# Moving a quarter of the first batch's turns and last transforms in among the first token tiles of a fused spectral mixing and feed-forward kernel

## The chip, the cores and the metric

The kernel runs on one core of one Trainium2 chip. The metric is the device time of one execution in microseconds (us). Before the change it is 847.4 us.

## The reference

There are two parts. The first transforms each of 8 batches of 3008 x 256 values along the sequence, multiplies by a complex 256 x 256 matrix, thresholds softly and transforms back. The second puts each of the resulting 24064 tokens through a feed-forward layer.

```python
X = np.fft.rfft(x, axis=1)
Yr = Xr @ w_r - Xi @ w_i + b_r          # Yi likewise
Yr = np.sign(Yr) * np.maximum(np.abs(Yr) - lam, 0.0)
y = np.fft.irfft(Y, n=x.shape[1], axis=1)
# ... y, as 24064 tokens of 256, is x of the second part
h = x @ w_in                            # 256 -> 2048
r = np.maximum(h, 0.0)
g = s * (r * r) + b
return (g @ w_out).astype(np.float32)   # 2048 -> 256
```

Since b is one number, b times the column sums of `w_out` is a vector of 256 that is added to each token. The kernel computes it once and calls it the bias.

## The kernel before

The transforms are matrix products on TensorE, whose results an eviction (`evac`) copies from a PSUM bank to SBUF. A running sum of estimated costs decides whether ScalarE or VectorE gets each eviction. Batch 0 goes first and alone. From then on the token tiles run, and the transforms of the next batch are laid between their matmuls by a plan of slots, 16 to a tile.

At the end of batch 0 stand the turns (a transposition by matmul, tile `vs`) and the last DFT (tile `yt`, which is what the token tiles read). `ec` is one of two halves of the 256 features, and the 32 values of `n2` go in groups.

```python
        # end of first_batch, for ec = 1
        for k in range(4):
            turn(1, k)                    # 8 values of n2: 8 matmuls, 2 evictions
            some(1)                       # one piece of batch 1's first DFT (tile u)
            if k:
                last_dft(1, 8 * (k - 1))
        last_dft(1, 24)
        return more
    # ...
    schedule(0, 10, more)
    plan.setdefault(15, []).append(make_bias)
    plan.setdefault(17, []).append(load_x_2)
```

A pair of slots of a token tile is four matmuls of 512 columns, a relu on ScalarE (tile `rt`) and a square (tile `gt`), mostly on VectorE. The gt then feed the second product (`psa`, then `ost`).

```python
        rt = rpool.tile([P, 2, 512], F32, name="rt", tag="rt")      # 3 buffers
        nc.scalar.activation(out=rt[:, :, 0:w], in_=ps[:, :, 0:w], func=AF.Relu)
        # ...
            nc.vector.tensor_tensor(
                out=gt[:, :, 0:w], in0=rt[:, :, 0:w], in1=rt[:, :, 0:w], op=ALU.mult
            )
```

The bias needs the sum of `w_out` over its 16 row blocks. GpSimd adds them in SBUF, eight operations in a row, once `w_out` has come from memory. `make_bias` is one matmul with ones and two evictions.

```python
    def emit_load_weights():
        for dc in range(DC):
            nc.gpsimd.dma_start(out=w_in_t[dc], in_=moe_w_in[dc * P : (dc + 1) * P, :])
        nc.gpsimd.dma_start(
            out=w_out_t, in_=moe_w_out.rearrange("(mc p) d -> p mc d", p=P)
        )
    # ...
    def sum_w_out():
        acc = opool.tile([P, 2, D], F32, name="acc", tag="ost")
        nc.gpsimd.tensor_tensor(
            out=acc, in0=w_out_t[:, 0:2], in1=w_out_t[:, 2:4], op=ALU.add
        )
        for q in range(4, MC, 2):
            nc.gpsimd.tensor_tensor(out=acc, in0=acc, in1=w_out_t[:, q : q + 2], op=ALU.add)
        nc.gpsimd.tensor_tensor(out=w_sum, in0=acc[:, 0], in1=acc[:, 1], op=ALU.add)

    def make_bias():
        ps = other_bank()
        nc.tensor.matmul(ps[:, 0:D], ones, w_sum, start=True, stop=True)
        # ... two evictions with scale b
```

Of the kernel before, what the change touches and what calls it, by code (L numbers as in the profile page):

```python
# [14 lines left out]
P = 128  # L15
# [81 lines left out]
def kernel(  # L97
# [13 lines left out]
    nc = tc.nc  # L111
# [7 lines left out]
    HW = N2 // 2  # L119
# [45 lines left out]
    def evac(dst, src, cols, scale=None):  # L165
        ta, td = 0.17 + cols / 1200.0, 0.15 + cols / 960.0
        if load["act"] + ta <= load["dve"] + td:
            load["act"] += ta
            if scale is None:
                return None, nc.scalar.copy(out=dst, in_=src)  # L170
            return None, nc.scalar.mul(out=dst, in_=src, mul=scale)
        load["dve"] += td
        if scale is None:
            return nc.vector.tensor_copy(out=dst, in_=src), None
        return nc.vector.tensor_scalar_mul(out=dst, in0=src, scalar1=scale), None
# [3 lines left out]
    def mix_bank():  # L179
        return pools["m"].tile([P, 512], F32, name="psm", tag="psm")  # L180
# [3 lines left out]
    def any_bank():  # L184

        turn_of[0] += 1
        if "h" in pools:
            return (other_bank, one_bank)[turn_of[0] % 2]()
        return (mix_bank, one_bank, mix_bank, other_bank)[turn_of[0] % 4]()
# [4 lines left out]
    def one_bank():  # L194
        return fpool.tile([P, 512], F32, name="psf", tag="psf")

    def other_bank():
        return apool.tile([P, 512], F32, name="psa", tag="psa")
# [54 lines left out]
    eye_t = cpool.tile([P, P], F16, name="eye_t")  # L253
# [102 lines left out]
    vs = {}  # L356
# [6 lines left out]
    def first_batch():  # L363
# [3 lines left out]
        for g in range(N2 // 4):  # L367
            c, h = divmod(g, 2)
            for dc in range(DC):
                ps = one_bank() if dc else mix_bank()  # L370
                with tc.issue_after(last_pe.ins):
                    for j in range(4):
# [4 lines left out]
                            start=True, stop=True,  # L377
# [35 lines left out]
        vt = bigpool.tile([P, DC, N2, 96], F16, name="vt", tag="corr")  # L413
# [3 lines left out]
        def mix(ec, u):  # L417

            g = vpool.tile([P, 4, 2, P], F16, name="g0", tag="v")
            gs[(ec, u)] = g  # L420
            for half in range(2):
                ps = mix_bank().rearrange("p (j r e) -> p j r e", j=2, r=2)
                for j in range(2):
                    q = 4 * u + 2 * half + j
                    for dc in range(DC):
                        nc.tensor.matmul(  # L426
                            ps[:, j], ut[:, dc, 4 * q : 4 * q + 4, :],
                            W_t[:, dc, :, ec * P : (ec + 1) * P],
                            start=(dc == 0), stop=(dc == DC - 1),
                        )  # L430
                if half:
                    nc.scalar.copy(out=g[:, 2:4], in_=ps)
                    load["act"] += 0.58
                else:
                    nc.vector.tensor_tensor(
                        out=g[:, 0:2], in0=ps,
                        in1=b_g[:, :, ec * P : (ec + 1) * P].unsqueeze(1).to_broadcast(
                            [P, 2, 2, P]
                        ),
                        op=ALU.add,  # L440
                    )
                    load["dve"] += 0.69
# [27 lines left out]
        def inv_dft(ec, u):  # L470
            ps = other_bank()
            z = zt.pop((ec, u))
            for j in range(4):
                nc.tensor.matmul(
                    ps[:, j * P : (j + 1) * P], z[:, j, :], T_t[:, 4 * u + j, :],
                    start=True, stop=True,
                )
            evac(
                vt[:, ec, :, 16 * u : 16 * u + 16],
                ps.rearrange("p (k n) -> p n k", n=N2), 512,  # L480
            )
# [1 line left out]
        for h in range(2):  # L483
            vs[(0, h)] = vspool.tile([96, HW, D], F16, name="vs", tag="vs")

        def turn(ec, k):
            for i in range(2):
                ps = any_bank() if ec else mix_bank()
                n = 8 * k + 4 * i
                for j in range(4):  # L490
                    nc.tensor.matmul(
                        ps[0:96, j * P : j * P + P], vt[:, ec, n + j, :], eye_t,
                        start=True, stop=True,
                    )
                h, n = divmod(n, HW)
                evac(
                    vs[(0, h)][:, n : n + 4, ec * P : (ec + 1) * P],
                    ps[0:96].rearrange("p (j e) -> p j e", e=P), 512,
                )

        yt = yts[0] = ypool.tile([P, DC, N2, 96], F16, name="yt", tag="yt")

        def last_dft(ec, n2):

            if ec or n2 >= 16:
                ps = [any_bank(), any_bank()]
            else:
                ps = [one_bank(), other_bank()]
            for j in range(8):
                h, k = divmod(n2 + j, HW)  # L510
                nc.tensor.matmul(
                    ps[j // 4][:, (j % 4) * 96 : (j % 4) * 96 + 96],
                    vs[(0, h)][:, k, ec * P : (ec + 1) * P], C_t,
                    start=True, stop=True,
                )
            for i in range(2):
                evac(
                    yt[:, ec, n2 + 4 * i : n2 + 4 * i + 4, :],
                    ps[i][:, 0:384].rearrange("p (j n) -> p j n", n=96), 384,
                )  # L520

        more = s1_units(1, True)

        def some(n):
            for _ in range(n):
                if more:
                    more.pop(0)()

        steps = [(ec, u) for ec in range(DC) for u in range(U)]
        for i in range(2 * U + 2):  # L530
            if i < 2 * U:
                mix(*steps[i])
            if 0 <= i - 1 < 2 * U:
                fwd_dft(*steps[i - 1])
            if 0 <= i - 2 < 2 * U:
                inv_dft(*steps[i - 2])
            k = i - U - 2
            if 0 <= k < 4:
                turn(0, k)
            for n in {1: (0,), 2: (8,), 4: (16, 24)}.get(k, ()):  # L540
                last_dft(0, n)
            if i >= 2 * U:
                some(3)
            if i == 9:

                gate = nc.gpsimd.tensor_copy(out=low[0:1, 0, 0:1], in_=vt[0:1, 1, 0, 0:1])
                with tc.issue_after(gate.ins):
                    make_w_g()
                    make_bounds()
                    sum_w_out()  # L550
        for k in range(4):
            turn(1, k)
            some(1)
            if k:
                last_dft(1, 8 * (k - 1))
        last_dft(1, 24)
        return more


    def s1_units(b, more_banks=False):  # L560

        ud = dpool.tile([96, N2, D], F16, name="ud", tag="ud")
        hold = {}

        def unit(i):
            c, j = divmod(2 * i, XCH)
            if j == 0:
                hold["u"] = upool.tile([P, XCH, D], F16, name="u", tag="u")
            ps = any_bank() if more_banks else one_bank()
            nc.tensor.matmul(  # L570
                ps[0:96, :], A_t[0:N1, :], x16[(b, c)][0:N1, j * D : (j + 2) * D],
                start=True, stop=True,
            )
            u = hold["u"]
            evac(u[0:96, j : j + 2, :], ps[0:96, :].rearrange("p (j d) -> p j d", j=2), 512)
            if j == XCH - 2:
                nc.sync.dma_start(
                    out=ud[:, c * XCH : (c + 1) * XCH, :], in_=u[0:96]
                )
            if i == N2 // 2 - 1:  # L580
                uv = ud.rearrange("k n d -> (k n) d").rearrange("(q p) d -> p q d", p=P)
                for q in range(4):
                    t = uspool.tile([P, 6, D], F16, name="us", tag="us")
                    nc.sync.dma_start(out=t, in_=uv[:, 6 * q : 6 * q + 6, :])
                    us[(b, q)] = t

        return [lambda i=i: unit(i) for i in range(N2 // 2)]
# [273 lines left out]
    plan = {}  # L861

    def schedule(start, span, units):
        for i, u in enumerate(units):
            plan.setdefault(start + (i * span) // len(units), []).append(u)

    with tc.tile_pool(name="psm", bufs=4, space=bass.MemoryType.PSUM) as pool:
        pools["m"] = pool
        more = first_batch()
    pools["h"] = ctx.enter_context(  # L870
        tc.tile_pool(name="psh", bufs=2, space=bass.MemoryType.PSUM)
    )
# [6 lines left out]
        if tl[0] == "main" and tl[2] == 0 or tl[0] == "wide" and tl[2] == (0, 0):  # L879
            mark[tl[1]] = i * MC  # L880
    schedule(0, 10, more)
    plan.setdefault(15, []).append(make_bias)
    plan.setdefault(17, []).append(load_x_2)
    schedule(24, 42, s23_units(1))
    schedule(mark[1] - 12, 16, s4_units(1))
    for b in range(2, B):
        s0, s1, s2 = mark[b - 2], mark[b - 1], mark[b]
        p = s1 - s0
        schedule(s0 + 40, p - 48, s1_units(b))
        p = s2 - s1  # L890
# [47 lines left out]
```

## Time and profile before

| | before |
|---|---|
| device time, median of 6 runs (lowest to highest) | 847.43 us (847.01 to 849.07) |
| first token matmul `psh` | 47.90 us |
| first relu `rt` | 49.10 us |
| first square `gt` | 50.15 us |
| batch 1's second DFT, first matmul `psf<-F_t,us` | 62.91 us |

The last line is a good landmark: everything that the change takes away lies before it, and about two thirds of what it puts in elsewhere (1.00 of 1.56 us of matmul by the prediction's count). A trace's zero is not quite fixed, however. The first turn of `ec` = 1 comes at 41.21 us in this trace, so differences between kernels are taken from that turn on.

The prediction shows the shares of the engines, the busy time by stretch and the chain. This is GpSimd's timeline around the end of batch 0. The columns of a timeline are start and duration in us, engine, line, operation, output<-inputs with shapes, and in brackets the idle time before it with what ended it.

```profile
40.67 1.15 POOL L340 TENSOR_TENSOR acc<-w_out_t 128x512 f32<-128x512 f16 x1 [4.95 <-DMA w_out_t<-in_moe_w_out_dram]
41.90 7.30 POOL L344 TENSOR_TENSOR acc<-acc,w_out_t 128x512 f32<-128x512 f32 x6
49.28 0.72 POOL L345 TENSOR_TENSOR w_sum<-acc 128x256 f16<-128x256 f32 x1
```

GpSimd waits 4.95 us for `w_out`, then adds without a pause and is done at 49.28 + 0.72 = 50.00 us.

### The profile page before, as it was taken

What the parts mean: (1) busy time and instruction counts of PE and PEld (TensorE: products, weight loads), DVE (VectorE), ACT (ScalarE), POOL (GpSimd) and SP (SyncE); (2) the same over time, 40 slices, a digit from 0 to 9 for tenths busy, and PEclk for the clock granted to TensorE, in tenths of its full rate; (3) what the DMA queues carried; (4) which work ended last, traced back from release to release, by engine and by line L of the source; (5) the groups of instructions that cost most, each with busy time, mean ns of one, the idle gap of its engine ahead of it and who ended that gap; (6) DMA issues with size and microseconds to landing.
All of it is one profiled execution on the core that took longest, in us unless ns stands there. A gap on an engine that the chain in (4) does not pass through costs nothing.

```text
span 845.0 us, 17114 instructions
## 1 busy us (share of the span) xinstructions
PE 833.8 (99%) x6653; PEld 599.6 (71%) x6653; DVE 693.6 (82%) x1026; ACT 641.8 (76%) x864; POOL 45.0 (5%) x71
## 2 busy tenths in 40 slices
PE   8999999999999999999999999999999999999997
PEld 6857767777677766777677776777667777766765
DVE  5989987888888987888888888798978888776674
ACT  5988887778778877787777787778877878766673
POOL 5331000000000001000000000000000000000000
PEclk9999999999999999999999999999999999999999
DMA  8945567124752367324761248513354223411111
GB/s 202 180 143 122 121 173 203 57 77 101 203 154 56 101 169 190 92 68 107 189 175 49 81 103 205 160 42 91 113 144 125 64 74 95 112 33 38 38 44 50
DMA packets 105746, 96.06 MB, mean 114 GB/s; under 512 B 9542, under 2 KB 97482, under 8 KB 104322
## 3 DMA queue, kind: packets, MB, share of 16 engines
q1 hardware_dynamic: 99218, 80.55, 33.0%
q0 software_dynamic: 6448, 14.42, 10.6%
q8 instruction: 52, 0.85, 0.4%
q14 instruction: 28, 0.23, 0.1%
HBM read 53.52 MB, written 46.66 MB: 119 GB/s over the span
## 4 chain that ended last, share of the span: by engine, by line
PE 90%; ACT 3%; DMA 3%; DVE 2%; issue 1%; POOL 0%; SPq 0%; ACTq 0%; DVEq 0%; POOLq 0%
PE psa L840 37%; PE psh L769 36%; PE psf L635 4%; PE psf L570 2%; PE psf L621 2%; PE psf L606 2%; PE psf L665 2%; PE psf L718 2%; ACT rt L776 2%; PE psm L426 1%; DMA x<-in_x_dram 1%; DMA ud<-u 1%; DVE gt L783 1%; DMA us<-ud 1%; DMA F_c<-dft_fwd 0%
## 5 line engine op out<-in xcount | busy, mean ns | idle before, releaser
L776 ACT ACTIVATE rt<-psh 128x1024 f32<-128x1024 f32 (+2 forms) x384 | 386.7, 1008 | 119.6 <-PE psh L769 117.5
L783 DVE TENSOR_TENSOR gt<-rt 128x1024 f16<-128x1024 f32 (+2 forms) x322 | 385.7, 1202 | 95.4 <-ACT rt L776 94.5
L840 PE MATMUL psa<-w_out_t,gt 128*128 128x256 f16 (+1 forms) x3024 | 454.4, 272 | 0.1
L840 PEld LDWEIGHTS <-gt 128*128 128x128 f16 (+1 forms) x3024 | 300.9, 101 | 187.0 <-issue 1.4
L769 PE MATMUL psh<-yt,w_in 128*128 128x512 f16 (+1 forms) x1344 | 396.3, 378 | 0.2 <-ACT rt L776 0.2
L769 PEld LDWEIGHTS <-w_in 128*128 128x128 f16 x1536 | 142.8, 98 | 27.3 <-issue 1.8
L850 DVE SCALAR_TENSOR_TENSOR ost<-psa,s_bc,bias_bc 128x512 f32<-128x512 f32 (+2 forms) x97 | 71.1, 733 | 10.0 <-PE psa L840 8.2
L780 ACT ACTIVATE gt<-rt 128x1024 f16<-128x1024 f32 (+2 forms) x62 | 65.3, 1054 | 1.0
L640 DVE TENSOR_TENSOR ring<-psf,s 128x512 f16<-128x512 f32 x84 | 57.5, 685 | 3.8 <-PE psf L635 3.3
L170 ACT CAST v<-psf 128x512 f16<-128x512 f32 x78 | 45.3, 583 | 19.7 <-PE psf L665 19.7
L170 ACT CAST xf<-psf 128x512 f16<-128x512 f32 x82 | 47.9, 586 | 10.9 <-PE psf L606 10.9
L170 ACT CAST u<-psf 96x512 f16<-96x512 f32 x76 | 43.9, 580 | 12.4 <-PE psf L570 12.2
L769 PE MATMUL psh<-tail,w_in 128*128 128x512 f16 (+1 forms) x192 | 52.1, 353 | 0.0
L635 PE MATMUL psf<-W_g,xf 128*128 128x256 f16 x336 | 50.4, 273 | 0.0
L170 ACT CAST yt<-psf 128x480 f16<-128x480 f32 (+2 forms) x73 | 37.8, 525 | 11.6 <-PE psf L718 11.6
L213 POOL DMA_DIRECT2D x<-in_x_dram x36 | 18.7, 526 | 430.3 <-PE psf L570 429.2
L570 PE MATMUL psf<-x,A_t 94*96 94x512 f16 x103 | 39.3, 382 | 1.1 <-ACT yt L170 0.5
L646 DVE TENSOR_TENSOR ring<-ring,high 128x512 f16<-128x512 f16 x84 | 35.6, 423 | 2.3
L647 DVE TENSOR_TENSOR ring<-ring 128x512 f16<-128x512 f16 x84 | 35.5, 423 | 2.0
L645 DVE TENSOR_TENSOR ring<-ring,low 128x512 f16<-128x512 f16 x84 | 35.4, 421 | 1.6
L635 PEld LDWEIGHTS <-xf 128*128 128x128 f16 x336 | 32.9, 98 | 3.8
L718 PE MATMUL psf<-C_t,vs 96*128 96x96 f16 x448 | 33.2, 205 | 0.2 <-ACT yt L170 0.2
(97 smaller groups left out, 499.5 us busy)
## 6 DMA issues: line engine op xcount, KB each, us to landing
out_dram<-ost SPq DMA_DIRECT2D x152, 128.0 KB
ud<-u SPq DMA_DIRECT2D x28, 384.0 KB
us<-ud SPq DMA_DIRECT2D x28, 384.0 KB
vd<-v SPq DMA_DIRECT2D x42, 256.0 KB
vs<-vd SPq DMA_DIRECT2D x14, 768.0 KB
x<-in_x_dram POOLq DMA_DIRECT2D x28, 376.0 KB, 5.9
ring<-ring SPq DMA_DIRECT2D x280, 32.0 KB
out_dram<-ost SPq DMA_DIRECT2D x16, 120.0 KB
```

Source lines behind the costliest of these rows:

```text
L170: return None, nc.scalar.copy(out=dst, in_=src)
L570: nc.tensor.matmul(ps[0:96, :], A_t[0:N1, :], x16[(b, c)][0:N1, j * D : (j + 2) * D], start=True, stop=True,)
L635: nc.tensor.matmul(ps[:, r, :], xt[:, 2 - r, dc], W_g[:, dc, r], start=(dc == 0), stop=(dc == DC - 1),)
L640: nc.vector.tensor_tensor(out=t, in0=ps, in1=hold[i // 2][:, i % 2].unsqueeze(1).to_broadcast([P, 2, D]), op=ALU.add,)
L646: nc.vector.tensor_tensor(out=m, in0=m, in1=high, op=ALU.min)
L718: nc.tensor.matmul(ps[:, j * 96 : (j + 1) * 96], vs[(b, h)][:, k, ec * P : (ec + 1) * P], C_t, start=True, stop=True,)
L769: nc.tensor.matmul(o, w_in_t[dc][:, mc * P : (mc + 1) * P], r, start=(dc == 0), stop=(dc == DC - 1),)
L776: nc.scalar.activation(out=rt[:, :, 0:w], in_=ps[:, :, 0:w], func=AF.Relu)
L780: nc.scalar.activation(out=gt[:, :, 0:w], in_=rt[:, :, 0:w], func=AF.Square)
L783: nc.vector.tensor_tensor(out=gt[:, :, 0:w], in0=rt[:, :, 0:w], in1=rt[:, :, 0:w], op=ALU.mult)
L840: nc.tensor.matmul(ps[0:size, h, :], gts[(ti, mc // 2)][:, mc % 2, sub * size : (sub + 1) * size], w_out_t[:, mc, :], start=(mc == 0), sto ...
L850: nc.vector.scalar_tensor_tensor(out=ost[0:size, 0:k], in0=ps[0:size, 0:k], scalar=s_bc[0:size], in1=bias_bc[0:size, 0:k], op0=ALU.mult, o ...
```

## The change

The intent is to let the token tiles begin earlier. For `ec` = 1 the turns and last DFTs of the second half of `n2` leave the end of batch 0, where the engines that empty PSUM are the bound, and are laid into slots 12 to 31, where TensorE has other matmuls to do. (`schedule(12, 22, rest)` spreads the eight groups over the 22 slots from 12 on.) The bias moves from slot 15 to slot 17.

```diff
-        for k in range(4):
-            turn(1, k)
-            some(1)
-            if k:
-                last_dft(1, 8 * (k - 1))
-        last_dft(1, 24)
-        return more
+        turn(1, 0)
+        turn(1, 4)
+        some(1)
+        turn(1, 8)
+        turn(1, 12)
+        some(1)
+        last_dft(1, 0)
+        last_dft(1, 4)
+        some(2)
+        last_dft(1, 8)
+        last_dft(1, 12)
+
+        rest = []
+        for n in (16, 24):
+            rest += [lambda n=n: turn(1, n), lambda n=n: turn(1, n + 4)]
+            rest += [lambda n=n: last_dft(1, n), lambda n=n: last_dft(1, n + 4)]
+        return rest, more
 ...  (turn and last_dft now do 4 values of n2 a call instead of 8; same matmuls, same evictions)
     schedule(0, 10, more)
-    plan.setdefault(15, []).append(make_bias)
-    plan.setdefault(17, []).append(load_x_2)
+    schedule(12, 22, rest)
+    plan.setdefault(17, []).append(make_bias)
+    plan.setdefault(18, []).append(load_x_2)
```

More of the change, by code (lines that the diff above doesn't have):

```diff
@@ L484, in first_batch, with turn, last_dft @@
             vs[(0, h)] = vspool.tile([96, HW, D], F16, name="vs", tag="vs")
-        def turn(ec, k):
-            for i in range(2):
-                ps = any_bank() if ec else mix_bank()
-                n = 8 * k + 4 * i
-                for j in range(4):
-                    nc.tensor.matmul(
-                        ps[0:96, j * P : j * P + P], vt[:, ec, n + j, :], eye_t,
-                        start=True, stop=True,
-                    )
-                h, n = divmod(n, HW)
-                evac(
-                    vs[(0, h)][:, n : n + 4, ec * P : (ec + 1) * P],
-                    ps[0:96].rearrange("p (j e) -> p j e", e=P), 512,
-                )
+        def turn(ec, n):
+            ps = any_bank() if ec else mix_bank()
+            for j in range(4):
+                nc.tensor.matmul(
+                    ps[0:96, j * P : j * P + P], vt[:, ec, n + j, :], eye_t,
+                    start=True, stop=True,
+                )
+            h, k = divmod(n, HW)
+            evac(
+                vs[(0, h)][:, k : k + 4, ec * P : (ec + 1) * P],
+                ps[0:96].rearrange("p (j e) -> p j e", e=P), 512,
+            )
         yt = yts[0] = ypool.tile([P, DC, N2, 96], F16, name="yt", tag="yt")
-        def last_dft(ec, n2):
-            if ec or n2 >= 16:
-                ps = [any_bank(), any_bank()]
-            else:
-                ps = [one_bank(), other_bank()]
-            for j in range(8):
-                h, k = divmod(n2 + j, HW)
+        def last_dft(ec, n):
+            if ec or n >= 16:
+                ps = any_bank()
+            else:
+                ps = other_bank() if n % 8 else one_bank()
+            for j in range(4):
+                h, k = divmod(n + j, HW)
                 nc.tensor.matmul(
-                    ps[j // 4][:, (j % 4) * 96 : (j % 4) * 96 + 96],
+                    ps[:, j * 96 : j * 96 + 96],
                     vs[(0, h)][:, k, ec * P : (ec + 1) * P], C_t,
@@ L515, in last_dft @@
                 )
-            for i in range(2):
-                evac(
-                    yt[:, ec, n2 + 4 * i : n2 + 4 * i + 4, :],
-                    ps[i][:, 0:384].rearrange("p (j n) -> p j n", n=96), 384,
-                )
+            evac(
+                yt[:, ec, n : n + 4, :],
+                ps[:, 0:384].rearrange("p (j n) -> p j n", n=96), 384,
+            )
         more = s1_units(1, True)
@@ L538, in first_batch @@
             if 0 <= k < 4:
-                turn(0, k)
-            for n in {1: (0,), 2: (8,), 4: (16, 24)}.get(k, ()):
+                turn(0, 8 * k)
+                turn(0, 8 * k + 4)
+            for n in {1: (0, 4), 2: (8, 12), 4: (16, 20, 24, 28)}.get(k, ()):
                 last_dft(0, n)
@@ L868 @@
         pools["m"] = pool
-        more = first_batch()
+        rest, more = first_batch()
     pools["h"] = ctx.enter_context(
```

## The prediction

> **What bounds the kernel now.** First the page's busy shares, then the shares of the chain that ended last.
>
> ```profile
> PE 833.8 (99%) x6653; PEld 599.6 (71%) x6653; DVE 693.6 (82%) x1026; ACT 641.8 (76%) x864; POOL 45.0 (5%) x71
> ...
> PE 90%; ACT 3%; DMA 3%; DVE 2%; issue 1%; POOL 0%; SPq 0%; ACTq 0%; DVEq 0%; POOLq 0%
> ```
>
> TensorE is the bound. The change neither adds nor removes a matmul, so it can only gain what TensorE loses in gaps. The 99% does not show those: a matmul is drawn longer than its turn in the pipeline. I therefore took starts, not lengths, from TensorE's timeline: eight 512-column matmuls from 47.90 to 49.62 us are 0.216 us each, and likewise 0.108 for 256 columns, 0.055 for 128 and 0.0425 for 96. Gap = distance between starts minus these. From 72 to 824 us it comes to 0.6 to 1.5 us per 40 us where no records are missing, mostly rounding. Where batch 0 ends it is denser: 0.8 us in 40.0 to 42.1, 0.3 to 44.3, 1.1 to 46.6, 0.4 to 49.6, 0.4 to 52.0: 3.1 us in 12. From there to 63 us it is near zero. Then the busy time by stretch:
>
> ```profile
> core 0: us, PE busy (x) PEld busy (x) DVE busy (x) ACT busy (x) POOL busy (x), PEclk, DMA share, GB/s
> ...
> 38.00:48.00 10.00, 8.48 (x100) 5.94 (x100) 9.39 (x18) 8.99 (x20) 6.91 (x6) 1.00 0.43 101
> 48.00:59.50 11.50, 11.29 (x59) 5.44 (x57) 10.32 (x11) 10.66 (x15) 1.88 (x2) 1.00 0.56 164
> 59.50:63.00 3.50, 3.50 (x28) 2.47 (x28) 3.14 (x3) 2.04 (x3) 0.35 (x1) 1.00 0.54 141
> 63.00:90.00 27.00, 26.88 (x225) 19.93 (x224) 24.36 (x47) 22.83 (x33) 2.74 (x8) 1.00 0.50 106
> ```
>
> In 38 to 48 us VectorE and ScalarE are 94% and 90% busy emptying PSUM banks; TensorE waits for banks. The chain over that stretch says the same (start, us, what):
>
> ```profile
> 41.89 1.07 ACT vs L170 x2
> 42.96 0.49 ACT u L170
> 43.45 0.38 ACT yt L170
> 43.83 0.49 ACT vs L170
> 44.31 0.49 ACT u L170
> 44.80 0.49 ACT vs L170
> 45.29 0.49 ACT u L170
> 45.77 0.39 ACT yt L170
> 46.20 0.59 PE psa L570 x2
> ...
> 47.70 1.29 DVE u L174 x2
> ...
> 49.10 1.03 ACT rt L776
> ```
>
> Evictions of vs (turns), yt (last DFT) and u (first DFT of batch 1) stand back to back, and the first relu of the token tiles (rt) starts at 49.10. After that VectorE is the tight one for ten products:
>
> ```profile
> 50.15 11.48 DVE L783 TENSOR_TENSOR gt<-rt 128x1024 f16<-128x1024 f32 x10 [1.18 <-ACT rt L776]
> 61.99 1.23 DVE L783 TENSOR_TENSOR gt<-rt 128x1024 f16<-128x1024 f32 x1 [0.36 <-ACT rt L776]
> ```
>
> Tile 0 cannot use its second product freely until its eight gt exist (50.15 + 8 x 1.15 = 59.3 us); from then TensorE is truly the bound, because a pair of slots holds 4 x 0.216 + 8 x 0.108 = 1.73 us of matmul against 1.15 of VectorE and 0.97 of ScalarE.
>
> **What the Trainium skill says.** The page "Perfetto Trace Analysis", section "Identifying the Most-Contended Engine", says matmul busy time is no measure of distance to the roofline, because matmuls are pipelined. This trace agrees: 8.48 of 10 us busy in 38 to 48 while the starts leave 2.8 us of gap. "TensorE: Matmul & The Clock Gate", section "Wait — 56ns, not 53.3ns?", gives 55.6 and 215.7 ns start to start at 128 and 512 columns; the trace has 55 and 215 to 216. "PSUM — Partial Sum Buffer", section "Engine vs sequencer instructions", says the queues of ScalarE and VectorE are strict FIFO and matmuls start in program order. So a bank that waits behind other evictions holds up TensorE, and an eviction moved among the tokens delays every gt behind it. The trace's 11.48 us block of gt, and TensorE's longest wait here (0.52 us before 46.20, for ScalarE's yt), fit that.
>
> **The change part by part.** Moved: for the second half of e and n2 = 16 to 31, four turns and four last-DFT groups: 16 matmuls of 0.055 and 16 of 0.0425, 0.88 + 0.68 = 1.56 us of TensorE, and 8 evictions. An eviction's turn on its engine (distance between starts) is 0.60 (vs) or 0.46 us (yt) on VectorE and 0.48 or 0.38 on ScalarE. Splitting the two functions into groups of four changes no count.
>
> *Taken from the end of batch 0.* I compared the built instruction orders. VectorE's list from 43.94 us on was 2 vs, 4 yt, 2 u (4.25 us) and becomes 3 u, 1 yt (2.26). ScalarE loses 2 vs, 1 yt and 1 u (1.8 us). I then walked the new order by hand with the durations above, each bank free when its eviction ends: TensorE reaches the last u at about 45.1, the first token matmul at 45.3 (was 47.90); ScalarE finishes its u at 46.1; four matmuls plus 0.2 us give the first rt at 46.5 (was 49.10). So the token stage starts 2.6 us earlier. TensorE had 1.56 us less to do there, so 2.6 - 1.56 = 1.0 us of gap is gone. Of the 2.6 us, the eviction load explains 1.9 (3.8 us over two engines); the other 0.7 are two bank waits of TensorE (0.28 us for vs, 0.52 us for yt) which lose their cause.
>
> *Put into the token tiles.* Same walk, counted from the first rt. ScalarE and VectorE set the pace of tile 0, and two turns and two last-DFT groups stand between its matmuls. VectorE takes one vs after its fourth gt: counting them from 0, gt 7 ended at about +10.2 (59.3) and ends at +10.8. ScalarE takes a vs and a yt, and the two bias evictions now follow (0.38 + 0.83 us) before rt 8. The 32nd second product of tile 0 came at +13.8 and comes at +14.9: 1.05 later, for 1.00 us of moved matmuls (three turns, two groups) ahead of it. So TensorE pays for almost all that it takes in: the gaps in this stage were already filled with second products. In time from the start: 62.9 becomes 46.5 + 14.9 = 61.4, 1.5 us earlier, with 0.56 us (one turn, two groups) still to come. Net: 1.5 - 0.56 = about 1.0 us.
>
> *Bias at slot 17.* Same matmul and two evictions, later. Its w_sum is ready at 50.0 us; by the walk the matmul stands at 54.9, so no new wait. Its user, the first ost, comes at about 62. Nothing.
>
> *Afterwards.* 63 to 90 us: VectorE was busy 24.4 of 27.0 us (90%), ScalarE 22.8 (85%). Roughly four of the moved evictions (vs and yt on each) land at its beginning, where TensorE loses 0.5 us to an xf that is behind gt and ost; in the new order the same wait remains (0.57 by the walk). I allow 0.1 us more. Expected: 847.4 - 1.0 + 0.1 = 846.5 us.
>
> **Rivals.**
> 1. *The whole advance counts.* If token tiles absorbed the moved matmuls in idle time, the gain would be 2.6 us: 844.8. For it: TensorE has about 0.7 us of gap in 49.6 to 52. Against it: from 52 to 63 starts follow one another with no gap, so there is nothing to absorb 1.56 us.
> 2. *VectorE becomes the bound of tiles 0 to 2.* Its queue is full for 11.5 us and 90% full afterwards; three more evictions (0.60 + 0.60 + 0.46 us) might each appear as delay of gt, then of second products: +1.7 us on top, total about 848. Against it: once tile 0 has its gt, TensorE has 48 second products (5.2 us) in reserve.
> 3. *Banks.* The two psa banks also hold the sums of the second product. A turn or last DFT that takes one must be evicted before the next pair of sub-tiles needs it, and one turn waits for the ost that frees its bank. If these meet badly, 0.5 to 1 us is lost: 847 to 847.5. In the walk ost ends 0.6 us before that turn, which is little.
> 4. *Data.* The fourth chunk of u needs the buffer of the first, whose store to memory is issued at 40.94; the last such store took about 2.6 us to land. It is needed at 45.1 instead of 47.05. If late, half a microsecond goes.
>
> **Range and chances.** The central figure is 846.5. Rivals 2 to 4 push up by 0.3 to 1.5 us, rival 1 down by up to 1.6; balancing of ScalarE against VectorE also differs after the change, so later tiles shift by a few tenths either way. The three runs before spread 0.5 us. Range 845.4 to 847.7. Two per cent is 17 us, more than the whole batch-0 end; faster or slower by that has chance 0.005 each.
>
> **What would show it right or wrong.** First token matmul (psh) at 45.3 and first rt at 46.5 us; VectorE's idle before its first gt similar; the stretch up to it with fewer vs and yt evictions. Batch 1's second DFT (psf<-F_t,us) beginning at 61.4 instead of 62.91, followed by one turn and two groups. TensorE's gaps by starts about 1 us less in 40 to 48 and unchanged after. I am wrong if TensorE shows waits for gt, vs or psa between 50 and 70 us (rivals 2 and 3), if the last u waits (4), or if that second landmark is 2 us or more earlier (1).

## The result, and the profile after

| | before | after |
|---|---|---|
| device time, median of 6 (lowest to highest) | 847.43 us (847.01 to 849.07) | 849.14 us (848.67 to 849.82) |
| ratio, 95% interval | | 1.0019 [1.0006, 1.0032] |

A ratio is the mean time of one kernel's runs over that of the other's of the same rounds, so it is not quite the ratio of the medians. By the 2% measure the two are the same; the interval says that the changed kernel is slightly slower. That is 1.7 us more by the medians, where 0.9 us less was predicted, and outside the range.

The page of the changed kernel, first its busy shares, then the shares of the chain that ended last:

```profile
PE 834.2 (98%) x6653; PEld 599.3 (71%) x6653; DVE 695.9 (82%) x1027; ACT 642.4 (76%) x863; POOL 47.5 (6%) x71
...
PE 91%; DVE 3%; ACT 3%; DMA 1%; issue 1%; POOL 0%; ACTq 0%; DVEq 0%; POOLq 0%
```

The matmuls are the same 6653. GpSimd (POOL) is 2.5 us busier with the same 71 instructions. VectorE (DVE) is 2.3 us busier. Its mix of work has changed a little (1027 instructions instead of 1026), but experiment 1 below has the same 1027 in 693.9 us, so 2.0 us of this is longer durations. The chain holds 3% of DVE instead of 2%.

The stretches of busy time, with the columns of the prediction's table. The cuts are at the first token matmul (45.5), at the first second products and at the landmark (63.60):

```profile
38.00:45.50 7.50, 6.76 (x67) 4.30 (x68) 7.50 (x14) 7.01 (x16) 4.18 (x4) 1.00 0.65 139
45.50:52.50 7.00, 6.83 (x38) 3.34 (x37) 5.58 (x5) 6.37 (x9) 6.36 (x5) 1.00 0.41 125
52.50:63.60 11.10, 9.51 (x66) 5.82 (x66) 10.44 (x10) 8.31 (x13) 3.40 (x7) 1.00 0.56 147
```

The first row ends 2.4 us earlier than before, as intended. The last row is where the loss shows: TensorE is busy 9.51 of 11.10 us, a stretch for which the prediction had near zero gap. VectorE is 94% busy with 10 instructions there. In the second row GpSimd works 6.36 of 7.00 us, until 52.17, and VectorE's gt begin within it, at 47.80; in the kernel before GpSimd had 1.88 us of work from 48 us on, and none from the start of gt at 50.15 to the end of that stretch at 59.5.

The chain from the end of batch 0 on (start, us, what) answers to the one that the prediction shows of before:

```profile
45.71 0.88 PE psh L778 x4
...
46.74 1.03 ACT rt L785
...
47.80 6.59 DVE gt L792 x4
54.39 0.60 DVE vs L174
54.99 4.55 DVE gt L792 x4
...
59.58 0.39 PE psa L849 x2
```

The matmuls and the first relu are where the prediction put them, 46.74 for an expected 46.5. Then four gt take 6.59 us, and the next four 4.55. The path runs straight through VectorE until TensorE at last gets gt for a second product at 59.58. So it is the first four gt that are too long, and each of them can be looked at alone. VectorE's timeline, from narrow windows:

```profile
47.80 1.68 DVE L792 TENSOR_TENSOR gt<-rt 128x1024 f16<-128x1024 f32 x1 [1.43 <-ACT rt L785]
...
49.41 2.17 DVE L792 TENSOR_TENSOR gt<-rt 128x1024 f16<-128x1024 f32 x1
...
51.50 1.75 DVE L792 TENSOR_TENSOR gt<-rt 128x1024 f16<-128x1024 f32 x1
```

And what GpSimd does at that time, first its six additions together, then the last two of them alone, then the last sum:

```profile
42.31 8.19 POOL L344 TENSOR_TENSOR acc<-acc,w_out_t 128x512 f32<-128x512 f32 x6
...
47.25 1.16 POOL L344 TENSOR_TENSOR acc<-acc,w_out_t 128x512 f32<-128x512 f32 x1
...
48.48 2.02 POOL L344 TENSOR_TENSOR acc<-acc,w_out_t 128x512 f32<-128x512 f32 x1
...
50.58 1.59 POOL L345 TENSOR_TENSOR w_sum<-acc 128x256 f16<-128x256 f32 x1
```

An undisturbed gt is 1.22 us long and an undisturbed add 1.15, and the last sum was 0.72 in the kernel before. Read the two lists against each other. The gt at 47.80 begins under the add that ends at 47.25 + 1.16 = 48.41, 0.61 us later. The add at 48.48 ends at 50.50 although it needs only 1.15; the gt that was running ended at 47.80 + 1.68 = 49.48, so it waited 1.00 for it. The gt at 49.41 then stands until that add ends at 50.50, that is 1.09 us, and needs 1.08 more. The sum at 50.58 stands until the gt ends at 51.58, and the gt at 51.50 until the sum ends at 52.17. The two engines take turns, each waiting out what is left of the other's operation. What each gt needs after that is the same: 1.68 - 0.61 = 1.07, then 1.08, then 51.50 + 1.75 - 52.17 = 1.08 us (a little less than the 1.22 of an undisturbed one; why is not shown). That speaks for waiting and against running slowly side by side. The three gt together are (1.68 - 1.22) + (2.17 - 1.22) + (1.75 - 1.22) = 1.94 us too long.

Nothing of this shows as a wait: the operations are drawn longer, as busy time. The waits appear one engine further on. The waits that fit, in 44 to 110 us (total us, times, longest):

```profile
PE psh L778 <- ACT rt L785: 1.2, 4, 0.6
...
ACT rt L785 <- DVE gt L792: 0.9, 2, 0.6
...
PE psa L849 <- DVE gt L792: 0.5, 1, 0.5
```

A late gt keeps one of the three rt buffers, so the next relu starts late, so its PSUM banks are not free for the next psh. By starts, TensorE's gaps are 1.2 us between 51.9 and 54.4 and 0.7 us just before 59.58. The landmark comes at 63.60 instead of the predicted 61.4.

**What the page "SBUF — State Buffer" says of it.** The Trainium skill's section "SBUF: two separate sides" calls the second pair of SBUF interfaces, which VectorE shares with GpSimd, an exclusive lock: a VectorE operation with two SBUF inputs takes it against a GpSimd operation that reads SBUF, and the later one blocks fully. The turns above agree: the add stands 1.00 us and the gt 1.09 us, by the reading above in each case until the other's operation has ended. The prediction had not looked this page up.

### The profile page after: what moved, and what is told of

Read it like the earlier page. It is cut to its first block, busy times and chain, and to the rows that moved or that the text cites. A ratio compares the mean times of both kernels' runs of the same rounds, so it can differ in the third digit from the quotient of the medians. Undisturbed runs are those within 1.5% of the kernel's fastest.

```text
span 847.0 us, 17109 instructions
## 1 busy us (share of the span) xinstructions
PE 834.2 (98%) x6653; PEld 599.3 (71%) x6653; DVE 695.9 (82%) x1027; ACT 642.4 (76%) x863; POOL 47.5 (6%) x71
## 4 chain that ended last, share of the span: by engine, by line
PE 91%; DVE 3%; ACT 3%; DMA 1%; issue 1%; POOL 0%; ACTq 0%; DVEq 0%; POOLq 0%
PE psa L849 37%; PE psh L778 36%; PE psf L644 4%; PE psf L579 3%; PE psf L630 2%; PE psf L615 2%; PE psf L727 2%; PE psf L674 2%; DVE gt L792 2%; ACT rt L785 1%; PE psm L426 1%; DMA x<-in_x_dram 1%; DMA F_c<-dft_fwd 1%; PE psf L456 0%; ACT yt L170 0%
## 5 line engine op out<-in xcount | busy, mean ns | idle before, releaser
L789 ACT ACTIVATE gt<-rt 128x1024 f16<-128x1024 f32 (+2 forms) x64 | 67.3, 1051 | 1.0
L170 ACT CAST u<-psf 96x512 f16<-96x512 f32 x80 | 46.3, 580 | 12.8 <-PE psf L579 12.5
L170 ACT CAST xf<-psf 128x512 f16<-128x512 f32 x77 | 45.0, 586 | 9.7 <-PE psf L615 9.6
```

Of the source, the lines that this page charges most:

```text
L170: return None, nc.scalar.copy(out=dst, in_=src)
L789: nc.scalar.activation(out=gt[:, :, 0:w], in_=rt[:, :, 0:w], func=AF.Square)
```

## The experiments

The theory: gt and GpSimd's sum of `w_out` exclude each other; the change moved gt into the sum, and this costs about 2 us. Rival A: VectorE is overloaded by the moved evictions (the prediction's second rival). Rival B: the places of the moved groups or of the bias among the slots cause the loss. Each kernel was timed in 5 rounds against the kernel before. In the first four the medians of before were 847.56 us (846.90 to 849.26, 9 runs), in the next four 847.53 (846.79 to 848.07), in the last three 847.39 (846.70 to 849.29).

### 1. The sum out of the way, by loading `w_out` first

```diff
     def emit_load_weights():
-        for dc in range(DC):
-            nc.gpsimd.dma_start(out=w_in_t[dc], in_=moe_w_in[dc * P : (dc + 1) * P, :])
         nc.gpsimd.dma_start(
             out=w_out_t, in_=moe_w_out.rearrange("(mc p) d -> p mc d", p=P)
         )
+        for dc in range(DC):
+            nc.gpsimd.dma_start(out=w_in_t[dc], in_=moe_w_in[dc * P : (dc + 1) * P, :])
```

This is the changed kernel with `w_out` loaded before the two halves of `w_in` instead of after them. GpSimd can add earlier. The traces of the two kernels list the same instructions in the same order on TensorE, VectorE and ScalarE.

> The changed kernel with the order of three loads turned round: w_out before the two halves of w_in. Instruction order on every compute engine is unchanged; only GpSimd's sum of w_out can start earlier. Theory A (GpSimd's sum and VectorE's gt products shut each other out): the sum ends before the first gt at 47.8 us, the first four gt take 4.6 us together instead of 6.59, and the time falls by about 2.3 us from 849.1 to about 846.8, ratio to before about 0.9993. Theory B (the moved evictions and matmuls themselves overload VectorE and ScalarE in tile 0): time stays at 849, ratio 1.002. Theory C (the new loads order delays w_in beyond the first token matmul at 45.5 us): slower than 849.

Measured: correct, 847.03 us (846.72 to 847.08), ratio to before 0.9992 [0.9978, 1.0005]. GpSimd's timeline:

```profile
36.03 1.15 POOL L340 TENSOR_TENSOR acc<-w_out_t 128x512 f32<-128x512 f16 x1
37.25 7.31 POOL L344 TENSOR_TENSOR acc<-acc,w_out_t 128x512 f32<-128x512 f32 x6
44.64 0.72 POOL L345 TENSOR_TENSOR w_sum<-acc 128x256 f16<-128x256 f32 x1
```

VectorE's, at the same place as above:

```profile
48.05 4.67 DVE L792 TENSOR_TENSOR gt<-rt 128x1024 f16<-128x1024 f32 x4 [1.43 <-ACT rt L785]
```

And the stretches after the first token matmul, to the landmark at 61.94:

```profile
45.80:52.50 6.70, 6.53 (x38) 3.27 (x37) 5.27 (x6) 6.28 (x10) 0.00 (x0) 1.00 0.42 128
52.50:62.00 9.50, 9.47 (x70) 5.96 (x68) 8.84 (x9) 8.16 (x13) 1.73 (x7) 1.00 0.62 167
```

The sum ends at 45.36, 2.7 us before the first gt. Each operation is at its plain length again: four gt 4.67 us instead of 6.59. TensorE is busy 9.47 of 9.50 us where it was 9.51 of 11.10. From the first token matmul to the landmark it takes 61.94 - 45.80 = 16.14 us, against 63.60 - 45.55 = 18.05 in the changed kernel. The difference of 1.91 us is what the meeting of the two engines cost, and nearly all of the 2.1 us by which the median falls. The evictions are all still there and in the same places, so rival A falls, and so does rival B as the cause of this loss.

### 2. No sum at all

```diff
     def sum_w_out():
-        acc = opool.tile([P, 2, D], F32, name="acc", tag="ost")
-        ...  (the eight additions)
+        nc.gpsimd.tensor_copy(out=w_sum, in_=w_out_t[:, 0])
```

The changed kernel, with loads as they were. It is wrong (relative error 0.60), as the bias is then false.

> The changed kernel without GpSimd's eight additions over w_out; a copy of one block stands for the sum, so the bias and the result are wrong on purpose. Theory A: first four gt take 4.6 us, time about 846.8 as for the other order of loads. Theory B: 849.

Measured: 846.94 us (846.66 to 847.09), ratio 0.9992 [0.9980, 1.0005]. VectorE's timeline:

```profile
47.72 4.67 DVE L792 TENSOR_TENSOR gt<-rt 128x1024 f16<-128x1024 f32 x4 [1.43 <-ACT rt L785]
```

The same 4.67 us and the same time as in experiment 1, by another way. So it is the sum that costs, and not the order in which the weights arrive.

### 3. The meeting made in the kernel before

```diff
         nc.gpsimd.tensor_tensor(out=w_sum, in0=acc[:, 0], in1=acc[:, 1], op=ALU.add)
+        for _ in range(2):
+            nc.gpsimd.tensor_tensor(out=acc, in0=acc, in1=w_out_t[:, 0:2], op=ALU.add)
```

Two more additions after the sum, whose result nobody uses, in the kernel before. They fall under its first gt.

> The kernel before, with two more GpSimd additions (1.15 us each, result not used) behind the sum, so that GpSimd reads SBUF until about 52.3 us instead of 50.0, while gt starts at 50.15. Nothing waits for them. Theory A: the first two or three gt are held up by about 2 us in all, and the time rises by 1 to 2.5 us over before, to 848.5 to 850. Theory B: no change, 847.4.

Measured: correct, 849.73 us (849.11 to 850.03), ratio 1.0024 [1.0012, 1.0037]. GpSimd's two additions, then VectorE's ten gt, which took 11.48 us in the kernel before:

```profile
51.37 4.11 POOL L347 TENSOR_TENSOR acc<-acc,w_out_t 128x512 f32<-128x512 f32 x2
...
50.73 13.79 DVE L785 TENSOR_TENSOR gt<-rt 128x1024 f16<-128x1024 f32 x10 [1.18 <-ACT rt L778]
```

The waits of TensorE for gt:

```profile
PE psa L842 <- DVE gt L785: 1.8, 3, 0.8
```

Two operations on an engine that is nearly idle make the kernel before 2.2 us slower by the medians, with no change to TensorE, VectorE or ScalarE. The ten gt are 2.31 us longer, and the additions 2.02 us each (with 0.08 us between them) instead of 1.15. This reproduces the loss without the change.

### 4. The exchanged loads alone

The edit of experiment 1, in the kernel before.

> The kernel before with w_out loaded first. Its sum ended 0.15 us before the first gt anyway. Theory A and B: no change, 847.2 to 847.5. It tells whether the order of loads is worth something by itself; if it is faster than 847.0, the gain of the changed kernel with this order would not be all due to the collision.

Measured: correct, 847.33 us (846.97 to 848.07), ratio 0.9999 [0.9986, 1.0011]. The order of the loads by itself is worth nothing that these runs resolve (the interval is about 1 us to each side). What experiment 1 won back, it won by parting the sum from gt.

### 5. GpSimd busy, but only writing

```diff
         nc.gpsimd.tensor_tensor(out=w_sum, in0=acc[:, 0], in1=acc[:, 1], op=ALU.add)
+        for _ in range(6):
+            nc.gpsimd.memset(acc, 0.0)
```

> The kernel before with six GpSimd memsets of 128x512 fp32 behind the sum, in place of the two extra additions of the earlier run. They keep GpSimd busy under the first gt products too, but read nothing from SBUF. If it is the reads of GpSimd that shut out a VectorE product with two SBUF inputs, the first ten gt take 11.5 us as before and the time is 847.5. If any GpSimd work does it, the ten gt take over 12.5 us and the time is 848.5 or more.

Measured: correct, 847.46 us (846.97 to 847.96), ratio 0.9998 [0.9984, 1.0012]. GpSimd's memsets and VectorE's ten gt:

```profile
50.44 3.44 POOL L347 MEMSET acc<- 128x512 f32 x6
...
50.14 11.53 DVE L785 TENSOR_TENSOR gt<-rt 128x1024 f16<-128x1024 f32 x10 [1.19 <-ACT rt L778]
```

The memsets lie wholly under gt, and the ten take 11.53 us, as before. So it is not that GpSimd is busy; of the two kinds of work tried, the one that reads SBUF costs and the one that only writes it does not. The Trainium skill's "SBUF — State Buffer", section "Who interferes with whom", says just this: a VectorE instruction with two SBUF inputs contends with a GpSimd instruction that reads SBUF, not with one that only writes it. Experiments 3 and 5 agree, 13.79 against 11.53 us. The section also exempts operations with at most one SBUF input outside the fast modes. That too fits: the evictions of vs and u from PSUM that VectorE does under the sum in 41 to 47 us take 0.68 us each, and the vs at 54.31 us in the changed kernel, after the sum, takes 0.68 too.

### 6 to 8. The bias, the places of the moved groups, half the move

All three start from experiment 1, so that the meeting is out of the way. By the code of `schedule` the eight groups stand in slots 17 to 29 in experiment 7 and 4 to 23 in experiment 9; the expectations give wider ranges, also for the changed kernel (12 to 31).

```diff
 # 6: the bias where it was
-    plan.setdefault(17, []).append(make_bias)
+    plan.setdefault(15, []).append(make_bias)
 # 7: the moved groups later and closer
-    schedule(12, 22, rest)
+    schedule(17, 14, rest)
 # 8: only n2 = 24 to 31 moves, 16 to 23 stays at the end of batch 0
-        for n in (16, 24):
+        turn(1, 16)
+        turn(1, 20)
+        last_dft(1, 16)
+        last_dft(1, 20)
+        for n in (24,):
```

> The changed kernel with w_out loaded first (847.0 us) and the bias product back at slot 15. The sum is ready at 45.4 us, long before. If the bias's place is of no account, as the prediction said, 846.8 to 847.3. If its two evictions on ScalarE hold up rt, slower by up to 0.8 us.

Measured (6): correct, 846.91 us (846.43 to 847.64), ratio 0.9992 [0.9979, 1.0004]. The place of the bias makes no difference that these runs resolve.

> The changed kernel with w_out loaded first, and the moved turns and last DFTs in slots 17 to 31 instead of 12 to 34, so that fewer of them meet the stage where VectorE and ScalarE set the pace and none is left for the end of the stretch. If the remaining 0.4 us lost after 62 us are their evictions, it moves by some tenths: 846.6 to 847.4. If evictions in tile 0 were the main cost of the change, it gains 1 us or more: under 846.2.

Measured (7): correct, 846.92 us (846.78 to 846.98), ratio 0.9991 [0.9978, 1.0003]. Nor do these slots.

> The changed kernel with w_out loaded first, and only the half for n2 = 24 to 31 moved; the half for 16 to 23 stays at the end of batch 0. By the gap account half the gain is left: first token matmul about 1.2 us later than with all moved, time 847.2 to 847.4. If the move of evictions into the tokens costs more than it gains, it is faster than 847.0.

Measured (8): correct, 847.84 us (847.69 to 848.14), ratio 1.0003 [0.9990, 1.0015]. This is a miss: half the move was expected to give part of the gain, and gives none. Its first token matmul comes 6.20 us after the first turn, where the kernel before has 6.69 and the full move 4.24. Half the work taken away brings 0.49 us of the 2.45. The advance is thus not proportional to what is moved. The trace says where it went. One of the moved turns runs at 47.57 us, still before the first token matmul at 47.79, and so does one more piece of batch 1's first DFT than in the other two kernels. TensorE's gaps by starts, from the first turn to the first token matmul, are 1.70 us, where the kernel before has 1.84 and experiment 1 has 0.95. Why the gaps stay is open: no run takes the remaining evictions apart.

### 9 and 10. Earlier slots, and the two small variants together

```diff
 # 9, from experiment 1: the moved groups from slot 4 on
-    schedule(12, 22, rest)
+    schedule(4, 22, rest)
 # 10, from experiment 1: 6 and 7 together
-    schedule(12, 22, rest)
-    plan.setdefault(17, []).append(make_bias)
+    schedule(17, 14, rest)
+    plan.setdefault(15, []).append(make_bias)
```

> The changed kernel with w_out loaded first and the moved units in slots 4 to 25, earlier by eight, so that all eight evictions fall in tile 0 and none beyond 62 us. VectorE takes three of them (1.66 us) before its eighth gt instead of one (0.60). If the few tenths still missing from the predicted gain are lost after 62 us, and tile 0 has room, 846.5 to 846.9. If VectorE's pace in tile 0 counts, the second products start about 1 us later and the time is 847.4 or more.

Measured (9): correct, 847.01 us (846.71 to 847.03), ratio 0.9992 [0.9979, 1.0004]. This is the same as experiment 1, and hits neither of the two expectations. With the meeting out of the way, a first slot of 4, 12 or 17 makes no difference that these runs resolve. That is one more point against rival B.

> The changed kernel with w_out loaded first, the moved units in slots 17 to 31 and the bias at slot 15: both small variants at once. Each alone gave 846.9. No more than a tenth or two is expected: 846.7 to 847.0.

Measured (10): correct, 846.75 us (846.40 to 846.90), ratio 0.9989 [0.9976, 1.0003]. This is the lowest median of all. With five runs a kernel the lowest of several like medians may be chance. It is 2.4 us below the changed kernel's median and 0.6 us below that of the kernel before, though the interval of the latter ratio still includes 1.

### 11. The sum on TensorE

```diff
     def make_bias():
         ps = other_bank()
-        nc.tensor.matmul(ps[:, 0:D], ones, w_sum, start=True, stop=True)
+        for mc in range(MC): nc.tensor.matmul(ps[:, 0:D], ones, w_out_t[:, mc], start=mc == 0, stop=mc == MC - 1)
 ...
-                    sum_w_out()
```

The changed kernel, without any GpSimd sum; 16 matmuls do it instead of one.

> The changed kernel with the loads in their old order and no GpSimd sum: TensorE sums w_out itself by 16 products of 256 columns with ones. The collision is gone as with w_out loaded first (847.0), but TensorE has 15 more products of 0.108 us: 1.6 us more, 848.6 us. If TensorE had idle time there, under 848.

Measured: correct, 848.90 us (848.22 to 850.32), ratio 1.0017 [1.0004, 1.0029]. VectorE's gt, then TensorE's sum:

```profile
47.66 4.67 DVE L792 TENSOR_TENSOR gt<-rt 128x1024 f16<-128x1024 f32 x4 [1.43 <-ACT rt L785]
...
54.87 1.91 PE L349 MATMUL psa<-w_out_t,ones 128*128 128x256 f16 x16
```

The gt are free, but 15 more matmuls of 0.108 us are 1.6 us on the engine that bounds the kernel. Its landmark comes 63.09 - 41.16 = 21.93 us after the first turn; in experiment 1 it is 61.94 - 41.56 = 20.38, so 1.55 us go to the matmuls. This is the same size of loss by another cause. GpSimd is the right place for the sum, if it runs early.

## Why the prediction was wrong

**The step that failed** is the pace of gt in "Put into the token tiles": "counting them from 0, gt 7 ended at about +10.2 (59.3) and ends at +10.8." Counted so from the first rt, gt 7 ends at +12.8 us in the changed kernel (59.52 - 46.74), and at +10.9 in experiment 1, where GpSimd's sum is out of the way. The walk used one constant turn of 1.15 us for each gt, taken from a trace in which the two engines happened to miss each other by 0.15 us.

What hid it is the paragraph "Bias at slot 17": "Its w_sum is ready at 50.0 us; by the walk the matmul stands at 54.9, so no new wait. [...] Nothing." It looks at GpSimd only as the producer of w_sum, and takes 50.0 us from the trace as a fixed time. It does not ask what VectorE does meanwhile. By the prediction's own count the first rt comes 2.6 us earlier; with the old distance of 1.05 us from rt to gt, the first gt stands at about 47.6, and GpSimd reads until 50.0. The overlap was there to be seen. It cost 1.92 us of gt (6.59 against 4.67) and 1.91 us of path.

None of the four rivals was it. The second had VectorE become the bound, but by evictions. It gave the right engine, and a time nearer to the measured one (848), for the wrong reason, which is luck: experiments 1 and 2 keep every eviction and lose the delay. Among the signs that would prove it wrong, the prediction did name waits of TensorE for gt between 50 and 70 us. They came (0.5 us for gt, 1.2 us through rt).

The table sets the other steps against the runs. Experiment 1 is the changed kernel without the meeting. Times in brackets count from the first turn of `ec` = 1.

| | before | predicted | after | experiment 1 |
|---|---|---|---|---|
| first token matmul, us | 47.90 (6.69) | 45.3 | 45.55 (4.24) | 45.80 (4.24) |
| first rt | 49.10 | 46.5 | 46.74 | 47.00 |
| first rt to landmark | 13.81 | 14.9 | 16.86 | 14.94 |
| landmark | 62.91 (21.70) | 61.4 | 63.60 (22.29) | 61.94 (20.38) |

**Taken from the end of batch 0: right.** The first token matmul advances by 6.69 - 4.24 = 2.45 us, for 2.6 predicted.

**Put into the token tiles: right, once the meeting is gone.** From the first rt to the landmark experiment 1 takes 14.94 us, and the walk said 14.9. The moved matmuls cost 14.94 - 13.81 = 1.13 us there, for 1.05 predicted. So rival 1, that they would be free, was rightly dismissed.

**Bias at slot 17 by itself: right.** Experiment 6 puts it back and changes nothing that the runs resolve. In the changed kernel the sum ends at 52.17 us instead of 50.0, and the bias matmul comes at 55.99, so it still has no new wait.

**Banks and data (rivals 3 and 4): dismissed.** Experiment 1 has TensorE busy for 9.47 of 9.50 us in the tiles that would show it, and its first token matmul is on time.

**Afterwards: mis-sized.** The landmark of experiment 1 is 21.70 - 20.38 = 1.32 us early, with 0.56 us of moved matmuls still to come, so 0.76 us should remain. From the first turn to the end of the span it is (845.0 - 41.21) - (845.0 - 41.56) = 0.35 us. About 0.4 us is lost later, where 0.1 was allowed. Experiments 6, 7 and 9 do not bring it back. It is smaller than the spread of the runs of the kernel before, so its cause stays open. The gain of the idea is then some 0.5 us by the medians, and every interval of such a run still includes a ratio of 1.

**Slips in its working**, none of which changes the outcome: 1.5 - 0.56 is 0.94, not 1.0; the two bank waits of 0.28 and 0.52 make 0.80, not 0.7; rival 1 puts 0.7 us of gap into 49.6 to 52, where the first paragraph has 0.4 (the trace gives 0.4). And the 848 of the second rival lies outside the range that was to hold the rivals.

In sum, with the terms as measured: 847.4 - 0.76 + 0.4 + 1.9 = 848.9 us, and 849.14 was measured.

One thing could not be tried. With `schedule(22, 20, rest)` in experiment 1, which puts the moved groups into slots 22 to 39, the program does not build: the build ends with "Deadlock detected". In the code batch 1's ring takes over the buffer from which the turns read. That may be the cause; it was not checked.

## What to carry to other kernels

When a change makes a stage start earlier, look at what every engine does at that new time, also one that is 5% busy and on nobody's path: a duration taken from the old trace holds only for the old company. A VectorE product of two SBUF operands should not run beside GpSimd operations that read SBUF, and the cheapest remedy tried here was to start GpSimd's work sooner by changing the order of three loads. If the same operation takes 1.7 to 2.2 us at one place and 1.2 elsewhere, and no wait is shown, look for a lock, not for a queue.

## What the Trainium skill lacked or had wrong

- "SBUF — State Buffer", sections "SBUF: two separate sides" and "Who interferes with whom": right in kind, as experiments 3 and 5 show (ten gt in 13.79 and 11.53 us). It speaks of the later operation as the one that blocks, but has no case of two queues. Here both engines have operations in a row and take turns, so each loses: GpSimd's six additions are 8.19 us instead of 7.30, its last sum 1.59 instead of 0.72, and VectorE's four gt 6.59 instead of 4.67.
- "Perfetto Trace Analysis", section "Optimizing Scalar/DVE Operations", warns of the lock only for 2-port operations of VectorE. Here a plain product with two SBUF inputs is 0.46 to 0.95 us longer by it.
- "Perfetto Trace Analysis", section "Identifying the Most-Contended Engine", takes VectorE's occupancy as a fair measure of how close it is to its roofline. The time spent standing for GpSimd is drawn as busy: VectorE shows 695.9 us for 1027 instructions in the changed kernel, and 693.9 us for the same 1027 in experiment 1. No page that was read says that such a stand shows as duration and not as a wait.
